# Attention, gated unit and softplus layer in one planned program: other transfer times, and slack on every VectorE and ScalarE instruction, in the simulation that makes the order

## The chip, the cores and the metric

The kernel runs on one core of one Trainium2 chip. The metric is the device time of one execution in microseconds. Shown with the program are the times of three runs, and one further execution that the hardware profiler took.

## What is computed

Three layers follow one another over 4 x 576 = 2304 tokens of 512 features, all in float32.

```
scores = q k^T / 8                      # 4 batches, 8 heads, 576 tokens, 64 features
mask: heads 0-3: 0 <= i - j < 32;  heads 4-7: j <= i and j = i (mod 32)
x = softmax(masked scores) v            # to 2304 x 512
xn = x / sqrt(mean(x^2) + 1e-6) * rms_g
y = (silu(xn w_gate) * (xn w_val)) w_out    # 512 -> 1536 -> 512
out = softplus(y w_in) w_out2               # 512 -> 2048 -> 512
```

## The kernel before

**The work.** The attention goes by units: a batch, a pair of heads, and about half of its query blocks (local heads have blocks of 64 queries and 96 keys, strided heads have blocks of 54, three residue classes of 18 tokens). A unit has a stage of scores (matmuls into one of four PSUM banks, VectorE's maximum, lines 555 to 588), of exponentials (ScalarE, one instruction per block, line 599), of normalisation, of transposes (line 637) and of values (line 660). In the two wide layers every float32 operand is split into a high and a low part, each product takes three matmuls with float32r operands (line 434), and 2 x 2 blocks of activations and weights are combined by sums and differences so that seven products stand for eight (`quad`). Tokens are worked in two sides, the first 1024 and the other 1280; the first side of the gated layer begins beside the attention.

**The weights.** They come as 64-bit words of 512 KB a tile. `decode` loads such a tile (line 369, buffers `raw`, a ring of two), makes float32 of it with one ScalarE and three VectorE instructions (lines 370 to 378) and stores it to `w_kept` (line 379), from where later sides fetch it (line 382).

**The order.** Tile's own scheduling is off. `Program.add` records each instruction as a node: engine, a duration in ns, what it reads and writes, and for a transfer the number `kb`. `Program.emit` then simulates the chip: `Trial.run` is a list scheduler in which each engine takes, among the nodes that are ready, the one that is due first; due times go back from the wanted order of TensorE. It does this 8 times, each time with the wanted times moved towards those that came out, keeps the trial that ends first, and issues the instructions in that order. Each engine of the chip then works its list from the front. There are two such plans: the attention with the first ten column groups of the gated layer, and all the rest.

What the simulation charges: VectorE 68 + n / 0.96 ns for n columns; ScalarE 15 + n / 0.98, and 236 + 0.83 n for an exponential with its accumulator read; a change between kinds of matmul 125 ns. Some instructions may go to another engine where the simulation finds it better: evictions to VectorE in place of ScalarE, and two-operand instructions to GpSimd when at least 900 ns of VectorE work stand ahead (`BESIDE`). A transfer takes SyncE 650 ns to issue; its data occupy one common queue for 5 ns per KB (`kb`), which starts 400 ns after the issue or when the transfer ahead is through, and it has landed 1100 ns after that:

```python
self.landed = max(self.landed, at + 400) + nodes[i][4]   # nodes[i][4] = 5 * kb
ends[i] = self.landed + 1100
```

Line numbers are those of the kernel before; a helper's line (355, 434) stands for all its callers.

Of the kernel before, what the change touches and what calls it, by code (L numbers as in the profile page):

```python
# [47 lines left out]

HOP = {"PE": 210, "DVE": 175, "ACT": 240, "POOL": 90, "SP": 60}
WINDOW = 3413  # L50
TURNS, KEEP, SWITCH, LEAVE = 8, 0.5, 125, 4000


class Program:
# [14 lines left out]

    def add(self, eng, dur, fn, r=(), w=(), kb=0, alt=None, mode=0):  # L70
        i = len(self.nodes)
        port = eng in ("DVE", "POOL") and not any("bank" in x[0] for x in [*r, *w])
        deps = set()
        for (key, lo, hi), wr in [(x, False) for x in r] + [(x, True) for x in w]:
            old = self.seen.setdefault(key, [])
            keep = []
            for e in old:
                if e[0] < hi and lo < e[1]:
                    if wr or e[3]:
                        deps.add(e[2])  # L80
                    if wr and lo <= e[0] and e[1] <= hi:
                        continue
                keep.append(e)
            keep.append((lo, hi, i, wr))
            self.seen[key] = keep
        deps.discard(i)
        self.nodes.append((eng, dur, fn, deps, 5 * kb, self.side, port, alt, mode))
# [40 lines left out]
class Trial:  # L128
# [7 lines left out]
    def pe_time(self, at, dur, mode):  # L136
        while at >= self.edge:
            used = self.acc / WINDOW
            if self.rate == 1 and used < 0.36:
                self.rate = 2  # L140
            elif self.rate == 2 and used > 0.75:
                self.rate = 1
            self.acc, self.edge = 0.0, self.edge + WINDOW
        t = (dur + (SWITCH if mode != self.mode else 0)) * self.rate
# [4 lines left out]
    def run(self):  # L149
        nodes, new, succ, ready, due, free = self.nodes, self.new, self.succ, self.ready, self.due, self.free  # L150
        begin, ends = self.begin, self.ends
# [16 lines left out]
        def release(i):  # L168
            for q in queues(i):
                heapq.heappush(wait[q], (ready[i], i))  # L170

        def earliest(q, base):
            for h in (wait[q], avail[q]):
                while h and h[0][1] in begin:
                    heapq.heappop(h)
            if avail[q]:
                return max(base, min(ready[i] for _, i in avail[q] if i not in begin))
            return max(base, wait[q][0][0]) if wait[q] else None
# [19 lines left out]
        while len(ends) < len(new):  # L198
            best = None

            def offer(at, e, s=0):
                nonlocal best
                if at is not None and (best is None or at < best[0]):
                    best = (at, e, s)

            first = [(t, q) for q in modes for t in [earliest(q, free["PE"])] if t is not None]
            if first:
                t = min(first)[0]
                pick = min((take(q, t)[0] + (LEAVE if q != self.mode else 0), q) for u, q in first if u <= t)
                offer(t, "PE", pick[1])  # L210
            offer(earliest("ACT", free["ACT"]), "ACT", "ACT")
            offer(earliest("SP", free["SP"]), "SP", "SP")
            t0, t1 = earliest("DVE0", free["DVE"]), earliest("DVE1", max(free["DVE"], self.port))
            if t0 is not None and t1 is not None and t0 == t1:
                offer(t0, "DVE", "DVE0" if take("DVE0", t0) < take("DVE1", t1) else "DVE1")
            else:
                offer(t0, "DVE", "DVE0")
                offer(t1, "DVE", "DVE1")
            base = max(free["POOL"], self.port)
            t = earliest("FLEX", base)  # L220
            if t is not None:
                beside = max(0, free["DVE"] - t) + sum(nodes[i][1] for _, i in avail["DVE0"])
                if beside >= BESIDE:
                    offer(t, "POOL", "FLEX")
            offer(earliest("POOL", base), "POOL", "POOL")
            at, e, s = best
            _, i = take(s, at)
            heapq.heappop(avail[s])
            if nodes[i][0] != e:
                nodes[i] = (e, nodes[i][7][0], nodes[i][7][1]) + nodes[i][3:]  # L230
            begin[i] = at
            free[e] = at + (self.pe_time(at, nodes[i][1], nodes[i][8]) if e == "PE" else nodes[i][1])
            ends[i] = free[e]
            if nodes[i][6]:
                self.port = free[e]
            if e == "SP":
                self.landed = max(self.landed, at + 400) + nodes[i][4]
                ends[i] = self.landed + 1100
            for j in succ[i]:
                gap = 0 if e == "PE" == nodes[j][0] else HOP[e]  # L240
                ready[j] = max(ready[j], ends[i] + gap)
                left[j] -= 1
                if not left[j]:
                    release(j)
# [3 lines left out]
def attn_glu_softplus(  # L248
# [13 lines left out]
    nc = tc.nc  # L262
    pr = Program()

    def all_of(key):
        return (key, 0, 1 << 30)
# [4 lines left out]
    def act(n, fn, r, w, table=False):  # L271
        pr.add("ACT", 15 + n / 0.98, fn, r + ([all_of("table")] if table else []), w)
# [14 lines left out]
    def dma(kb, fn, r, w):  # L287
        pr.add("SP", 650, fn, r, w, kb=kb)
# [23 lines left out]
    id_sb = const.tile([128, 128], F32, name="id_sb")  # L312
# [48 lines left out]
    hold = []  # L361

    def decode(src, t, kt, keep):

        raw, kraw = raws.next()
        u, ku = cvu.next()
        words = raw.bitcast(U32).rearrange("p (n two) -> p n two", two=2)
        wlo, whi = words[:, :, 0], words[:, :, 1]
        dma(512, lambda: nc.sync.dma_start(out=raw, in_=src), hold, [kraw])
        act(512, lambda: nc.scalar.activation(t, whi.bitcast(F32), AF.Copy, scale=2.0 ** -112), [kraw], [kt])  # L370
        dve(512, lambda: nc.vector.tensor_scalar(out=u, in0=t.bitcast(U32), scalar1=0x80000000, scalar2=None,
                                                 op0=ALU.bitwise_and), [kt], [ku], True)
        dve(512, lambda: nc.vector.scalar_tensor_tensor(  # L373
            out=u, in0=wlo, scalar=29, in1=u, op0=ALU.logical_shift_right, op1=ALU.bitwise_or),
            [kraw, ku], [ku])
        dve(512, lambda: nc.vector.scalar_tensor_tensor(
            out=t.bitcast(U32), in0=t.bitcast(U32), scalar=3, in1=u,
            op0=ALU.logical_shift_left, op1=ALU.bitwise_or), [kt, ku], [kt])
        dma(256, lambda: nc.sync.dma_start(out=wk[keep], in_=t), [kt], [("wk", keep, keep + 1)])

    def fetch(t, kt, keep):
        dma(256, lambda: nc.sync.dma_start(out=t, in_=wk[keep]), [("wk", keep, keep + 1)], [kt])
# [95 lines left out]
    def attention(at, use):  # L478
# [3 lines left out]

        qks = ring(at, "qk", 3, [128, 2 * QW])
        mask = at.tile([128, MW], BF16, name="mask")
        dma(100, lambda: nc.sync.dma_start(out=mask, in_=masks), [], [all_of("mask")])
        vb = ring(at, "vb", 2, [128, 9, 128])
        eb = ring(at, "eb", EB, [128, 5 * LK])
        pp = ring(at, "pp", 2, [128, 6, 128])
# [32 lines left out]
        def load_v(u):  # L521
            b, p, t0, n = units[u]
            kp, nt = (LK, 9) if p < 2 else (128, 6)
            vt, (kv, _, _) = vb.next()
            src = vl[b, p] if p < 2 else vs[b, p - 2]
            vals[u // 2] = (vt, kv)
            dma(nt * (48 if p < 2 else 50), lambda: nc.sync.dma_start(out=vt[:kp, :nt, :], in_=src), [], [all_of(kv)])

        def half(u, h):
            o = h ^ (u % 2)  # L530
# [116 lines left out]
        def stage_v(u):  # L647
            b, p, t0, n = units[u]
            loc = p < 2
            r0, r1 = (0, LK) if loc else (64, 64 + SK) if t0 else (0, SK)  # L650
            v0 = t0 if loc else 0
            vt, kv = vals[u // 2]
# [3 lines left out]
            for a in range(n):  # L656
                t, kt = pts[a // 3]
                for h in range(2):
                    o = (2 * (a % 3) + (h ^ (u % 2))) * nq
                    pr.add("PE", 59, lambda a=a, h=h, o=o, t=t: nc.tensor.matmul(  # L660
                        xb[64 * h:64 * h + 64, a * nq:(a + 1) * nq], lhsT=vt[r0:r1, v0 + a, 64 * h:64 * h + 64],
                        rhs=t[r0:r1, o:o + nq], start=True, stop=True), [all_of(kv), kt],
                        [kx], mode=1 if loc else 3)
            g = rg_sb[:, p:p + 1]
            if loc:
# [3 lines left out]
                src = xb[:, :w]  # L669
# [6 lines left out]
            else:  # L676
# [3 lines left out]
                src = xb[:, :w].rearrange("p (c m) -> p c m", m=18)  # L680
# [297 lines left out]
    with tc.manual_schedule():  # L978
# [38 lines left out]
                fn(*args)  # L1017
            pr.side = False

        dma(64, lambda: nc.sync.dma_start(out=id_sb, in_=ident), [], [all_of("id")])  # L1020
        dma(2, lambda: nc.sync.dma_start(out=rg_sb, in_=rg), [], [all_of("rg")])
        for i in range(WARM):
            pr.add("PE", 400, lambda: nc.tensor.matmul(
# [102 lines left out]
        for side, (c0, c1, c4) in enumerate(SIDES):  # L1126
# [3 lines left out]
            for p in range(n2):  # L1130
                i = prep2(p, c4 is not None, "POOL" if p == 0 or side == 0 and p < 4 else "DVE")
# [86 lines left out]
```

## Time and profile before

| what | value |
|---|---|
| median of 3 runs | 899.95 us (899.71 to 902.26) |
| the profiled execution | 900.52 us |
| its span, first to last instruction | 898.7 us |
| TensorE, VectorE, ScalarE, GpSimd busy | 882.7, 712.9, 486.1, 28.1 us |
| instructions | 14075 |
| mean granted TensorE clock | 0.993 |

Busy time is the union of an engine's instructions, without its waits. PE is TensorE, PEld its weight loads, DVE VectorE, ACT ScalarE, POOL GpSimd, SP SyncE, which issues all transfers. The ends of matmuls are modelled, so TensorE's busy time can hold small pauses. In a row of groups, "bank<-pt,vb" names the tile written and those read.

### The profile page before, as it was taken

The numbers are of one execution on the slowest core, as the hardware profiler recorded it, in microseconds if no ns is written. First come the engines' busy times: TensorE is split into PE (matmuls) and PEld (weight loads), VectorE is DVE, ScalarE is ACT, GpSimd is POOL, SyncE is SP. The second block draws the span as 40 slices with busy tenths as digits, with TensorE's granted clock in tenths as the row PEclk, the third lists the DMA queues.
The fourth block names the chain that finished last, engine by engine and source line by source line (L and its number), as shares of the span: only waits on it lengthen the run. The fifth ranks groups of instructions, "written<-read, shape, count | busy, mean of one in ns | idle before, by whom it ended". The sixth has DMA issues, their size and how long they took to land.

```text
span 898.7 us, 14075 instructions
## 1 busy us (share of the span) xinstructions
PE 882.7 (98%) x5320; PEld 725.7 (81%) x5320; DVE 712.9 (79%) x1349; ACT 486.1 (54%) x999; POOL 28.1 (3%) x26
## 2 busy tenths in 40 slices
PE   7899999999999999999999999999999999999998
PEld 6567777778777888888888888888888888888886
DVE  4988898998599995888988799877798456676644
ACT  5987664545364675444545567544474655434331
POOL 0000010200000000000100100000000000000000
PEclk7999999999999999999999999999999999999999
DMA  7874667363040443344553025321114111111003
GB/s 254 263 228 146 205 205 224 124 214 106 13 141 23 151 152 105 134 146 140 183 154 104 2 85 178 137 71 48 47 47 153 36 47 48 47 32 39 1 1 117
DMA packets 41858, 102.18 MB, mean 114 GB/s; under 512 B 4800, under 2 KB 5568, under 8 KB 41792
## 3 DMA queue, kind: packets, MB, share of 16 engines
q1 hardware_dynamic: 41792, 101.31, 35.5%
q8 instruction: 41, 0.67, 0.3%
q14 instruction: 25, 0.20, 0.1%
HBM read 78.74 MB, written 22.54 MB: 113 GB/s over the span
## 4 chain that ended last, share of the span: by engine, by line
PE 67%; DVE 3%; issue 0%
PE bank L434 67%; DVE xs L901 1%; DVE ob L355 0%; DVE tb L355 0%; DVE xs L355 0%; DVE win L355 0%; DVE w L355 0%; DVE ssq L355 0%; DVE glx L355 0%; DVE xs L919 0%; DVE gv L355 0%; DVE ssq L868 0%; DVE gv L868 0%; DVE gl L355 0%
## 5 line engine op out<-in xcount | busy, mean ns | idle before, releaser
L434 PE MATMUL bank<-ob,win 128*128 128x512 f32 (+1 forms) x1560 | 430.8, 360 | 2.7 <-ACT ob L351 1.8
L434 PEld LDWEIGHTS bank<-ob,win 128*128 128x128 f32 x1560 | 283.4, 188 | 55.0 <-ACT ob L351 2.2
L434 PE MATMUL bank<-tb,win 128*128 128x512 f32 x672 | 232.8, 392 | 0.0
L434 PEld LDWEIGHTS bank<-tb,win 128*128 128x128 f32 x672 | 125.4, 188 | 22.9 <-DVE xs L901 0.4
L919 DVE TENSOR_TENSOR xs<-bank,xs 128x512 f32<-128x512 f32 x126 | 86.8, 689 | 45.7 <-PE bank L434 44.4
L405 ACT ACTIVATE win<-w 128x512 fp32r<-128x512 f32 (+1 forms) x136 | 83.4, 616 | 63.9 <-PE bank L434 32.7
L355 DVE TENSOR_TENSOR win<-w,win 128x512 fp32r<-128x512 f32 (+1 forms) x134 | 89.5, 673 | 15.6 <-ACT win L405 12.6
L434 PE MATMUL bank<-wout,ghx 128*128 128x512 f32 x304 | 100.0, 390 | 0.0
L434 PE MATMUL bank<-wout,gh 128*128 128x512 f32 x272 | 90.4, 390 | 0.0
L434 PE MATMUL bank<-ghx,wout 128*128 128x512 f32 x224 | 84.1, 394 | 0.0
L434 PE MATMUL bank<-gh,wout 128*128 128x512 f32 (+1 forms) x256 | 81.3, 356 | 0.5 <-DVE xs L901 0.4
L901 DVE TENSOR_TENSOR xs<-bank,xs 128x512 f32<-128x512 f32 (+1 forms) x100 | 62.2, 628 | 8.9 <-PE bank L434 8.1
L434 PEld LDWEIGHTS bank<-wout,ghx 128*128 128x128 f32 x304 | 56.9, 188 | 11.7
L434 PEld LDWEIGHTS bank<-wout,gh 128*128 128x128 f32 x272 | 50.9, 188 | 10.6
L816 ACT ACTIVATE gv<-bank 128x512 f32<-128x512 f32 x48 | 28.4, 592 | 48.1 <-PE bank L434 47.6
L434 PE MATMUL bank<-wout,glx 128*128 128x512 f32 x152 | 53.2, 389 | 0.0
L434 PEld LDWEIGHTS bank<-gh,wout 128*128 128x128 f32 x256 | 45.5, 189 | 9.0 <-DVE xs L901 1.4
L434 PEld LDWEIGHTS bank<-ghx,wout 128*128 128x128 f32 x224 | 41.9, 188 | 8.4 <-ACT ghx L856 0.2
L434 PE MATMUL bank<-wout,gl 128*128 128x512 f32 x136 | 47.7, 389 | 0.0
L373 DVE SCALAR_TENSOR_TENSOR cvu<-raw,cvu 128x512 uint32<-128x512 uint32 x68 | 46.6, 686 | 1.0
L355 DVE TENSOR_TENSOR w<-w 128x256 f32<-128x256 f32 x109 | 45.4, 416 | 0.9
L820 DVE TENSOR_TENSOR gv<-bank,gv 128x512 f32<-128x512 f32 x48 | 32.9, 685 | 16.0 <-ACT gv L816 9.0
(131 smaller groups left out, 1211.8 us busy)
## 6 DMA issues: line engine op xcount, KB each, us to landing
raw<-w SPq DMA_DIRECT2D x68, 512.0 KB, 4.1
w<-w_kept SPq DMA_DIRECT2D x56, 256.0 KB, 2.6
w_kept<-cvtx SPq DMA_DIRECT2D x26, 256.0 KB, 3.7
cvt<-w_kept SPq DMA_DIRECT2D x26, 256.0 KB, 2.7
w_kept<-w SPq DMA_DIRECT2D x24, 256.0 KB, 4.2
qk<-qk SPq DMA_DIRECT2D x8, 601.0 KB, 5.6
w_kept<-cvt SPq DMA_DIRECT2D x18, 256.0 KB, 3.5
cvtx<-w_kept SPq DMA_DIRECT2D x18, 256.0 KB, 2.8
```

Of the source, the lines that this page charges most:

```text
L355: pr.add("DVE", 68 + n / 0.96, lambda: getattr(nc.vector, name)(o, x, y), r, w, alt=(110 + n * 2.3, lambda: getattr(nc.gpsimd, name)(o, x, ...
L373: dve(512, lambda: nc.vector.scalar_tensor_tensor(out=u, in0=wlo, scalar=29, in1=u, op0=ALU.logical_shift_right, op1=ALU.bitwise_or), [kra ...
L405: act(n, lambda: nc.scalar.activation(h, t, AF.Copy), [kt], [reg(0, o + lo, o + hi)])
L434: lambda a=a, b=b, i=i, st=st, mv=mv: nc.tensor.matmul(o, lhsT=st[a], rhs=mv[b], start=(first and i == 0), stop=(last and i == m - 1), ski ...
L816: act(CH, lambda: nc.scalar.activation(o, y[0], AF.Copy), [y[1]], [ko])
L820: dve(CH, lambda: nc.vector.tensor_add(o[0], y[0], o[0]), [y[1], o[1]], [o[1]])
L901: dve(n, lambda: nc.vector.tensor_add(x, pb, x), [kp, kx], [kx])
L919: dve(DM, lambda: nc.vector.tensor_add(x, pb, x), [kp, kx], [kx])
```

## The change

Only numbers of the simulation are edited. Each VectorE and ScalarE node gets 20 ns more. The `kb` of several kinds of transfers changes, and with it the time in the common queue: a raw weight tile 512 to 340, a store to `w_kept` 256 to 170, values 48 to 31 a block (local) and 50 to 41 (strided), the mask 100 to 140, the identity 64 to 40; the fetch from `w_kept` stays at 256, q and k at 0.35 a column. The landing delay of 1100 ns becomes 2110 for a raw tile, 1460 for a store, 1260 for all else; the two are told apart by their time in the queue. A strided value matmul is charged 36 ns in place of 59. What the instructions do stays the same; their order, and the engine of those that have a choice, follow from the new simulation.

```diff
--- before.py
+++ after.py
@@ -48,6 +48,7 @@
 
 HOP = {"PE": 210, "DVE": 175, "ACT": 240, "POOL": 90, "SP": 60}
 WINDOW = 3413
+SLACK = 20
 TURNS, KEEP, SWITCH, LEAVE = 8, 0.5, 125, 4000
 
 
@@ -69,6 +70,7 @@
 
     def add(self, eng, dur, fn, r=(), w=(), kb=0, alt=None, mode=0):
         i = len(self.nodes)
+        dur += SLACK if eng in ("DVE", "ACT") else 0
         port = eng in ("DVE", "POOL") and not any("bank" in x[0] for x in [*r, *w])
         deps = set()
         for (key, lo, hi), wr in [(x, False) for x in r] + [(x, True) for x in w]:
@@ -235,7 +237,7 @@
                 self.port = free[e]
             if e == "SP":
                 self.landed = max(self.landed, at + 400) + nodes[i][4]
-                ends[i] = self.landed + 1100
+                ends[i] = self.landed + (2110 if nodes[i][4] == 1700 else 1460 if nodes[i][4] == 850 else 1260)
             for j in succ[i]:
                 gap = 0 if e == "PE" == nodes[j][0] else HOP[e]
                 ready[j] = max(ready[j], ends[i] + gap)
@@ -366,7 +368,7 @@
         u, ku = cvu.next()
         words = raw.bitcast(U32).rearrange("p (n two) -> p n two", two=2)
         wlo, whi = words[:, :, 0], words[:, :, 1]
-        dma(512, lambda: nc.sync.dma_start(out=raw, in_=src), hold, [kraw])
+        dma(340, lambda: nc.sync.dma_start(out=raw, in_=src), hold, [kraw])
         act(512, lambda: nc.scalar.activation(t, whi.bitcast(F32), AF.Copy, scale=2.0 ** -112), [kraw], [kt])
         dve(512, lambda: nc.vector.tensor_scalar(out=u, in0=t.bitcast(U32), scalar1=0x80000000, scalar2=None,
                                                  op0=ALU.bitwise_and), [kt], [ku], True)
@@ -376,7 +378,7 @@
         dve(512, lambda: nc.vector.scalar_tensor_tensor(
             out=t.bitcast(U32), in0=t.bitcast(U32), scalar=3, in1=u,
             op0=ALU.logical_shift_left, op1=ALU.bitwise_or), [kt, ku], [kt])
-        dma(256, lambda: nc.sync.dma_start(out=wk[keep], in_=t), [kt], [("wk", keep, keep + 1)])
+        dma(170, lambda: nc.sync.dma_start(out=wk[keep], in_=t), [kt], [("wk", keep, keep + 1)])
 
     def fetch(t, kt, keep):
         dma(256, lambda: nc.sync.dma_start(out=t, in_=wk[keep]), [("wk", keep, keep + 1)], [kt])
@@ -482,7 +484,7 @@
 
         qks = ring(at, "qk", 3, [128, 2 * QW])
         mask = at.tile([128, MW], BF16, name="mask")
-        dma(100, lambda: nc.sync.dma_start(out=mask, in_=masks), [], [all_of("mask")])
+        dma(140, lambda: nc.sync.dma_start(out=mask, in_=masks), [], [all_of("mask")])
         vb = ring(at, "vb", 2, [128, 9, 128])
         eb = ring(at, "eb", EB, [128, 5 * LK])
         pp = ring(at, "pp", 2, [128, 6, 128])
@@ -524,7 +526,7 @@
             vt, (kv, _, _) = vb.next()
             src = vl[b, p] if p < 2 else vs[b, p - 2]
             vals[u // 2] = (vt, kv)
-            dma(nt * (48 if p < 2 else 50), lambda: nc.sync.dma_start(out=vt[:kp, :nt, :], in_=src), [], [all_of(kv)])
+            dma(nt * (31 if p < 2 else 41), lambda: nc.sync.dma_start(out=vt[:kp, :nt, :], in_=src), [], [all_of(kv)])
 
         def half(u, h):
             o = h ^ (u % 2)
@@ -657,7 +659,7 @@
                 t, kt = pts[a // 3]
                 for h in range(2):
                     o = (2 * (a % 3) + (h ^ (u % 2))) * nq
-                    pr.add("PE", 59, lambda a=a, h=h, o=o, t=t: nc.tensor.matmul(
+                    pr.add("PE", 59 if loc else 36, lambda a=a, h=h, o=o, t=t: nc.tensor.matmul(
                         xb[64 * h:64 * h + 64, a * nq:(a + 1) * nq], lhsT=vt[r0:r1, v0 + a, 64 * h:64 * h + 64],
                         rhs=t[r0:r1, o:o + nq], start=True, stop=True), [all_of(kv), kt],
                         [kx], mode=1 if loc else 3)
@@ -1017,7 +1019,7 @@
                 fn(*args)
             pr.side = False
 
-        dma(64, lambda: nc.sync.dma_start(out=id_sb, in_=ident), [], [all_of("id")])
+        dma(40, lambda: nc.sync.dma_start(out=id_sb, in_=ident), [], [all_of("id")])
         dma(2, lambda: nc.sync.dma_start(out=rg_sb, in_=rg), [], [all_of("rg")])
         for i in range(WARM):
             pr.add("PE", 400, lambda: nc.tensor.matmul(
```

## Rows read from the trace of the kernel before

**Rows 1.** Page, first part: busy us, share of the span, instructions of each engine.

```profile
PE 882.7 (98%) x5320; PEld 725.7 (81%) x5320; DVE 712.9 (79%) x1349; ACT 486.1 (54%) x999; POOL 28.1 (3%) x26
```

**Rows 2.** Windows by stage: stretch, its length, busy us (instructions) per engine, clock, DMA, GB/s.

```profile
0.00:22.50 22.50, 17.69 (x282) 14.79 (x285) 11.01 (x40) 13.18 (x76) 1.61 (x6) 0.79 0.76 254
22.50:45.00 22.50, 18.72 (x328) 12.96 (x322) 21.46 (x60) 20.92 (x91) 0.00 (x0) 0.98 0.83 264
45.00:67.50 22.50, 20.94 (x218) 15.22 (x218) 18.87 (x46) 19.66 (x57) 0.00 (x0) 1.00 0.72 228
67.50:90.00 22.50, 21.66 (x167) 15.83 (x166) 20.01 (x43) 17.22 (x30) 1.29 (x1) 1.00 0.47 144
90.00:247.50 157.50, 157.10 (x1218) 124.36 (x1217) 134.34 (x269) 82.49 (x148) 12.06 (x9) 1.00 0.50 156
247.50:292.50 45.00, 44.23 (x188) 34.66 (x187) 44.78 (x79) 25.57 (x44) 2.70 (x2) 1.00 0.27 82
292.50:877.50 585.00, 584.96 (x2864) 493.86 (x2863) 452.03 (x803) 304.19 (x554) 10.44 (x8) 1.00 0.28 88
877.50:898.70 21.20, 17.36 (x77) 14.06 (x75) 10.43 (x16) 2.87 (x5) 0.00 (x0) 0.96 0.33 124
```

**Rows 3.** Chain of work that ended last: start us, us, what.

```profile
272.56 0.60 DVE win L355
...
291.31 223.95 PE bank L434 x1172
...
515.30 379.58 PE bank L434 x1770
```

**Rows 4.** Waits of TensorE, 0 to 90 us: in total, times, longest.

```profile
PE bank L553 <- ACT eb L599: 3.3, 2, 2.9
PE bank L434 <- ACT ob L351: 1.8, 2, 1.4
PE bank L453 <- ACT eb L599: 1.4, 1, 1.4
...
PE bank L566 <- DMA qk<-qk: 0.7, 1, 0.7
```

**Rows 5.** Transfers issued at 20 to 75 us: count, KB each, median us to landing.

```profile
raw<-w SPq DMA_DIRECT2D x9, 512.0 KB, 4.0
vb<-v_loc SPq DMA_DIRECT2D x4, 432.0 KB, 6.3
vb<-v_str SPq DMA_DIRECT2D x4, 384.0 KB, 5.3
w_kept<-w SPq DMA_DIRECT2D x5, 256.0 KB, 5.4
qk<-qk SPq DMA_DIRECT2D x2, 608.0 KB, 6.7
qk<-qk SPq DMA_DIRECT2D x2, 601.0 KB, 7.0
w_kept<-cvt SPq DMA_DIRECT2D x1, 256.0 KB, 2.8
w_kept<-cvtx SPq DMA_DIRECT2D x1, 256.0 KB, 3.0
```

**Rows 6.** Window 20 to 75 us, columns as in rows 2.

```profile
20.00:75.00 55.00, 49.21 (x611) 34.64 (x611) 46.86 (x118) 49.03 (x174) 0.00 (x0) 0.97 0.75 237
```

**Rows 7.** Line 369, loads of raw weights, all 68.

```profile
DMA to landing us min/median/max: 3.2/4.1/7.8
```

**Rows 8.** Groups of instructions by line and form: the strided value matmuls.

```profile
L660 PE MATMUL bank<-pt,vb 54*64 54x54 f32 x352 | 9.0, 234 | 0.0
```

**Rows 9.** Waits of SyncE's queue: us in total, times, longest.

```profile
SPq L369 <- DVE cvu L373: 188.4, 58, 11.9
```

**Rows 10.** Two windows of the start, columns as in rows 2.

```profile
6.80:13.40 6.60, 2.98 (x108) 2.53 (x100) 4.68 (x15) 4.88 (x33) 0.00 (x0) 0.97 1.05 337
13.40:20.00 6.60, 6.46 (x94) 5.02 (x93) 4.63 (x19) 4.54 (x28) 0.00 (x0) 0.50 0.50 187
```

## The prediction

> **What bounds the kernel now.** I read the page's first part first: TensorE is busy 98% of the span, VectorE 79%, ScalarE 54% [rows 1]. A share over the whole span hides stages, so the busy time of each engine by stage came next [rows 2]. There the reader sees two kernels in one. From 292.5 to 877.5 us TensorE is busy 584.96 of 585.00 us at full clock; from 90 to 292.5 us it is idle 157.50 - 157.10 + 45.00 - 44.23 = 1.17 us. Only the first 90 us, the attention with the first weights decoded beside it, have room: 4.81 us idle up to 22.5 us, then 3.78, 1.56 and 0.84 us, together 10.99 us; 6.18 us of it lie between 22.5 and 90 us. The last 21.2 us hold 3.84 us, the tail behind the last matmul.
>
> The chain of work that ended last agrees [rows 3]: from 291.3 us on it is TensorE alone, 1172 + 1770 matmuls in two unbroken pieces, 223.95 us / 1172 = 191 ns and 379.58 us / 1770 = 214 ns each, short and long ones mixed. No order of the same matmuls shortens that. Just before it a run of VectorE instructions follows one another every 0.60 us.
>
> Third, what TensorE waited for in the first 90 us [rows 4]. The named waits are on ScalarE (the exponentials, the Square of the statistics, the splits of activations) and on VectorE; one, of 0.7 us, is on a transfer. So the place to win is the order of ScalarE's and VectorE's work before 90 us, and these two are themselves nearly full there: in 22.5 to 45 us VectorE has 1.04 us left and ScalarE 1.58 us, in 45 to 90 us 6.12 and 8.12 us [rows 2].
>
> **The change, part by part.** It edits only numbers by which the planner simulates; no instruction is added or removed in any kind. A number counts by the order it yields: the chip runs at its own speed, and each engine works in the order written.
>
> *Transfers.* Old charge per KB: 5 ns for most, for q and k 0.35 x 5 ns a column. I price the stretch 20 to 75 us by the transfers issued there [rows 5]. Nine raw weights x 512 x 5 = 2.56 us make 23.04; four local values x 9 x 48 x 5 = 2.16 make 8.64; four strided x 6 x 50 x 5 = 1.50 make 6.00; seven stores (5 + 1 + 1) x 1.28 make 8.96; four q-k loads at 2.13 (1216 columns) and 2.10 (1202 columns) make 8.46. Sum 55.1 us in a stretch of 55.0: in the plan the transfers are saturated there, so data are planned to come later and later. New: 9 x 1.70 + 4 x 1.395 + 4 x 1.23 + 7 x 0.85 + 8.46 = 15.30 + 5.58 + 4.92 + 5.95 + 8.46 = 40.2 us, 73%. The trace has the DMA engines at 0.75 in that stretch, 237 GB/s [rows 6]. So the new charge is right and the old one invented a queue. A raw weight alone is planned to land 0.40 + 2.56 + 1.10 = 4.06 us after its issue by the old numbers, 0.40 + 1.70 + 2.11 = 4.21 by the new; the row has 3.2 at least and 4.1 in the median [rows 7]. Alone nothing moves; behind others the new plan brings the data forward by up to 55.1 - 40.2 = 14.9 us summed over the stretch, less where a buffer has to come free first.
>
> What is that worth? Nothing directly, for transfers hardly stop TensorE. Indirectly: decoding is placed on ScalarE and VectorE where the plan thinks that the weight is there. Placed earlier it fills their gaps, and what follows it comes earlier. In 45 to 90 us both have room (6.12 and 8.12 us), so TensorE's 2.40 us of idle time could all go; in 22.5 to 45 us its 3.78 us could shrink by no more than the room of the fuller pair, 1.04 to 1.58 us. Lower bound 0, upper 2.40 + 1.58 = 3.98 us. I take the middle, 2.0 us, because room on an engine is not yet work that is ready for it.
>
> *Slack.* Each VectorE and ScalarE instruction is charged 20 ns more. A VectorE instruction over 512 columns was charged 68 + 512 / 0.96 = 601 ns; the chain shows one every 0.60 us [rows 3]. So the old charge was right and 621 is too long. Over the 60 + 46 + 43 = 149 VectorE instructions of 22.5 to 90 us [rows 2] the plan sees 3.0 us that don't exist; over ScalarE's 178 at most 3.6 us (an exponential and its accumulator read share one charge). The chip gives that time back as soon as it runs. What it changes is which work is held to be late: where the plan had no margin, it now has 20 ns for every instruction ahead. Good for: the 1.17 us of idle time in 90 to 292.5 us, which VectorE, full there (44.78 of 45.00 us), causes. Bad for: a fuller VectorE in the plan sends more subtractions to GpSimd. I put slack at 0, with bounds of 1.17 us gained and, for a loss, the new wait priced below.
>
> [...]
>
> *The strided value matmuls*, 59 ns charged before, 36 now. The row has 352 records [rows 8], two for each of 8 head pairs x 11 blocks x 2 halves = 176 charges; the plan loses 176 x 23 ns = 4.0 us of TensorE time over the attention. The row's 9.0 us / 176 = 51 ns lies between, 8 below the old and 15 above the new. Real TensorE time doesn't change by it; I take 0, bounds within those of the order. The other small charges (mask, identity, landing of stores and fetches later by 0.16 us in light traffic) move a plan that had spare time there: 0. If that cover went, the 0.7 us on a transfer [rows 4] is the nearest price.
>
> **Sum.** The profiled execution took 900.52 us, its span 898.7 with 1.82 around it; it lies 0.57 above the median, 899.95. I take the 2.0 us off the median: 897.95, say 898.0.
>
> **Rivals.**
>
> *Nothing comes of it.* The plan is truer, but in the raw buffers' ring of two the next load waits for VectorE anyway: 58 of the raw loads waited for the decoding instruction that frees their buffer, 188.4 us in all [rows 9]. Then transfers never were what set the decoding, the engines are as full as before, and the order changes only in detail. Against it: the plan's queue was saturated, which must have moved some decoding back. Time: 899.95.
>
> *A larger gain.* All idle time from 22.5 to 292.5 us goes, 6.18 + 1.17 = 7.35 us: 892.6. For it: every wait there is for ScalarE or VectorE work that a better order could have put first. Against it: VectorE busy 21.46 of 22.5 us. Half of it or more counts here, 896.3 and below.
>
> *Slower: a new wait in the attention.* With 20 ns more for every exponential and reduction, and weights planned earlier, a decoding step (about four instructions of 0.6 us) stands ahead of an exponential chain in ScalarE's or VectorE's order. TensorE's score matmuls then find no free bank. Its price is the longest such wait in the rows, 2.9 us [rows 4]: 899.95 + 2.9 = 902.9. It decides when it exceeds the 2.0 us won, that is with two decoding instructions or more on top of that. For it: ScalarE and VectorE are 93 to 95% full at 22.5 to 45 us, where each instruction put first delays another. [...]
>
> **How the numbers follow.** Within 0.3%, that is 2.7 us (897.25 to 902.65), a measurement of this kernel can hardly tell a change. The gain of about 2 us, my forecast, has 0.45; its own bounds are 899.95 - 3.98 = 896.0 and 899.4, so it splits into 0.20 faster and 0.25 within 0.3%. Nothing: 0.20, all within. The larger gain: 0.15, all faster. Slower: 0.20, of which 0.17 lie beyond the 0.3%. Faster 0.35, same 0.48, slower 0.17. For 8 in 10 the range reaches into both outer cases: low 893.5, short of the full 7.35 us; high 903.0, the new wait.
>
> **What would show it.** Right: from 22.5 to 90 us TensorE idle some 4 us instead of 6.18; raw loads and decodings earlier in that stretch; from 292 us on the same unbroken matmul chain, starting about 2 us earlier; the clock as before. The slack is right if the small waits at 247.5 to 292.5 us (0.77 us) shrink, wrong if GpSimd's busy time grows well above 28.1 us [rows 1] and VectorE waits for it. The forecast is wrong if idle time before 90 us is 11 us or more again, if a wait of 2 us or more stands at a score or statistics matmul, or if TensorE has idle time behind 292 us, where I left it none.

## The result

The changed kernel takes 906.80 us in the median of 5 runs (904.29 to 906.98) against 900.63 us (899.71 to 902.26, 5 runs) before: ratio 1.0057, 95% interval 1.0043 to 1.0071 (ratios here compare all executions, not the medians). It is slower, outside the range that I gave, and on the other side of the forecast. The profiled execution has a span of 904.9 us against 898.7.

The busy time by stage, changed kernel, columns and stretches as in [rows 2]:

```profile
0.00:22.50 22.50, 15.06 (x289) 13.18 (x289) 11.58 (x42) 13.36 (x76) 1.61 (x6) 0.92 0.90 307
22.50:45.00 22.50, 18.38 (x272) 12.94 (x274) 18.26 (x52) 19.10 (x78) 0.80 (x1) 0.81 0.68 219
45.00:67.50 22.50, 21.02 (x190) 16.01 (x182) 18.81 (x50) 15.67 (x54) 4.17 (x1) 0.81 0.55 171
67.50:90.00 22.50, 21.25 (x168) 14.75 (x167) 19.51 (x37) 17.36 (x32) 0.00 (x0) 1.00 0.63 199
90.00:247.50 157.50, 156.63 (x1230) 124.08 (x1231) 132.95 (x267) 83.22 (x149) 14.56 (x13) 1.00 0.48 154
247.50:292.50 45.00, 45.00 (x236) 36.68 (x231) 43.08 (x74) 26.08 (x44) 1.29 (x1) 1.00 0.25 76
292.50:877.50 585.00, 584.50 (x2860) 493.20 (x2859) 458.66 (x810) 306.88 (x559) 16.14 (x11) 1.00 0.28 88
877.50:904.90 27.40, 23.22 (x103) 18.89 (x101) 13.79 (x21) 3.54 (x6) 0.00 (x0) 0.97 0.26 96
```

TensorE's idle time in the first 90 us is 7.44 + 4.12 + 1.48 + 1.25 = 14.29 us; it was 10.99. The 6.2 us more of span divide so: 3.30 us of idle time in the first 90 us, 0.47 in 90 to 247.5 us, 0.46 behind 292.5, 0.34 in the tail, less 0.77 gained at 247.5 to 292.5; together 3.80 us. The other 2.4 us are busy time: 885.06 against 882.66 us for the same 5320 matmuls. The clock column goes with it: 0.81 in two stretches, where it was 0.98 and 1.00 (in the first 22.5 us it is the other way, 0.92 where it was 0.79).

Waits of TensorE from 0 to 90 us, changed kernel, as in [rows 4] (L555 starts a bank of scores with the mask, L639 is a transpose):

```profile
PE bank L555 <- ACT eb L601: 6.5, 3, 4.8
PE bank L639 <- DVE eb L357: 1.7, 1, 1.7
```

Its longest wait, for exponentials that free a bank of scores, went from 2.9 to 4.8 us. The chain of work that ended last, changed kernel, shows it and, much later, a second place:

```profile
7.96 1.43 ACT eb L601 x10
9.65 3.42 ACT eb L601 x21
13.11 0.54 PE bank L555 x2
...
423.69 4.59 DMA w_kept<-cvtx
...
432.42 468.31 PE bank L436 x2230
```

The chain waits through 31 ScalarE records (exponentials and accumulator reads) up to 13.11 us. At 432 us TensorE stood still for the 0.5 us that the last large window lacks; from there it is unbroken as in [rows 3].

The longer first wait goes with another order of the first two head pairs. TensorE's first score matmuls, before (96 columns: the local pair) and then changed (54 columns: the strided pair):

```profile
5.86 1.47 PE L566 MATMUL bank<-qk 64*64 64x96 f32 x36
```

```profile
5.87 1.08 PE L568 MATMUL bank<-qk 64*64 64x54 f32 x46
```

TensorE at half clock, changed kernel, three windows set on the stretches:

```profile
22.80:26.20 3.40, 3.15 (x61) 2.67 (x63) 2.25 (x11) 2.67 (x10) 0.00 (x0) 0.50 0.47 135
33.10:36.50 3.40, 3.40 (x5) 1.30 (x4) 2.23 (x6) 2.40 (x11) 0.00 (x0) 0.50 0.93 298
43.30:53.50 10.20, 9.28 (x55) 7.01 (x55) 10.20 (x24) 6.11 (x18) 4.97 (x1) 0.50 0.40 125
```

In the profiled execution of before there was one such stretch ahead of the tail, which [rows 10] show in part; the window set on the whole of it:

```profile
13.00:23.20 10.20, 10.06 (x154) 8.18 (x156) 7.18 (x25) 8.12 (x52) 0.00 (x0) 0.50 0.66 233
```

The changed kernel has one of its own between 12.6 and 16 us, and then these three more, with TensorE busy 3.15 + 3.40 + 9.28 = 15.83 us in them.

How much of this belongs to the order, and not to the one execution? Two kernels of the experiments, "second plan new" and "second plan, slack only", keep the first plan of before: in the first 90 us their matmuls, and their VectorE instructions, follow one another by tile names as before. Yet their profiled executions show half clock at 11.4 to 18.2 us (11.5 to 18.4) and once more at 45.5 to 48.9 (45.7 to 49.1). The second one, "second plan new":

```profile
45.50:48.90 3.40, 3.40 (x10) 2.67 (x9) 3.40 (x9) 2.29 (x11) 0.00 (x0) 0.50 0.51 111
```

So where half clock falls is not set by the order alone, and TensorE's busy time in the first 90 us, 79.01 us before, was 77.43 and 76.42 us in these two; a difference of two or three microseconds between two profiles can be one of executions, the 3.30 us above too. The sum of half clock separates the orders better: some 10.2 us in all three executions of the old first plan, 20.4 us in the changed kernel, 23.8 us in the other profiled execution of its first plan ("first plan new").

The six statistics matmuls show what half clock means. Timeline of TensorE, before:

```profile
30.19 3.12 PE L453 MATMUL bank<-gv,ones 128*128 128x512 f32 x6 [1.43 <-ACT eb L599]
```

and the same six in the changed kernel, line 455 there, where the granted clock is 0.50 from 33.1 to 36.5 us:

```profile
32.58 4.54 PE L455 MATMUL bank<-gv,ones 128*128 128x512 f32 x6 [1.19 <-ACT eb L601]
```

The sign that I gave for the transfers appeared. SyncE's timeline, first raw weights, before and then changed:

```profile
20.39 0.89 SPq L369 DMA_DIRECT2D raw<-w  x2
```

```profile
8.67 0.90 SPq L371 DMA_DIRECT2D raw<-w  x2
```

They are issued 12 us earlier, though not because a raw tile is charged less, as the experiments show. The decoding step on VectorE that reads the raw tile, its nine instructions in the first 90 us, first and last start, before and then changed:

```profile
L373 DVE SCALAR_TENSOR_TENSOR cvu<-raw,cvu x9: 677/692/693, 31.5 to 89.2; 128x512 uint32<-128x512 uint32 x9
```

```profile
L375 DVE SCALAR_TENSOR_TENSOR cvu<-raw,cvu x9: 675/692/693, 28.7 to 75.9; 128x512 uint32<-128x512 uint32 x9
```

The ninth starts 13 us earlier. So weights came sooner, and the attention beside them came later: its last value matmul starts at 248.0 us, before at 240.6.

### The profile page after: what moved, and what is told of

Its sections match the earlier page's. It is cut to its first block, busy times and chain, and to the rows that moved or that the text cites. A ratio compares the mean times of both kernels' runs of the same rounds, so it can differ in the third digit from the quotient of the medians.

```text
span 904.9 us, 14102 instructions
## 1 busy us (share of the span) xinstructions
PE 885.1 (98%) x5320; PEld 729.7 (81%) x5320; DVE 716.6 (79%) x1348; ACT 485.2 (54%) x994; POOL 38.6 (4%) x32
## 4 chain that ended last, share of the span: by engine, by line
PE 92%; DVE 4%; DMA 2%; ACT 1%; issue 0%; SPq 0%; ACTq 0%; DVEq 0%
PE bank L436 86%; PE bank L662 2%; PE bank L639 1%; PE bank L568 1%; PE bank L455 1%; ACT eb L601 1%; DMA raw<-w 1%; DMA w_kept<-cvtx 1%; PE bank L555 0%; DMA mask<-masks 0%; DMA vb<-v_loc 0%; DVE xs L474 0%; DVE cvu L375 0%; DVE mz L583 0%; DVE win L357 0%
## 5 line engine op out<-in xcount | busy, mean ns | idle before, releaser
L357 DVE TENSOR_TENSOR win<-w,win 128x512 fp32r<-128x512 f32 (+1 forms) x130 | 86.1, 667 | 20.2 <-ACT win L407 18.0
L436 PEld LDWEIGHTS bank<-gh,wout 128*128 128x128 f32 x256 | 45.5, 189 | 8.6 <-issue 0.9
```

The costliest lines, as they stand in the source:

```text
L357: pr.add("DVE", 68 + n / 0.96, lambda: getattr(nc.vector, name)(o, x, y), r, w, alt=(110 + n * 2.3, lambda: getattr(nc.gpsimd, name)(o, x, ...
L436: lambda a=a, b=b, i=i, st=st, mv=mv: nc.tensor.matmul(o, lhsT=st[a], rhs=mv[b], start=(first and i == 0), stop=(last and i == m - 1), ski ...
```

## The experiments

Theory A says that the new transfer numbers turned the first two head pairs round, and that this is the loss; theory B that the slack spoils the order; theory C that any newly made order lands some tenths of a per cent off. Each kernel was timed 5 to 12 times beside the kernel before on the same chip. For the kernels without idle matmuls, the table sets the ratio beside two readings of the first 90 us: TensorE's busy time and mean clock. The ratio comes from all executions, the readings from the single profiled one: before, "second plan new" and "second plan, slack only" share one first plan and read 76.42 to 79.01, and the 130 ns control's 0.98 is that of its fastest execution, with a granted clock of 0.998 over the span where the other ten had 0.994 to 0.996.

| kernel | ratio, 95% interval | busy in 0:90 | clock in 0:90 |
|---|---|---|---|
| before | 1 | 79.01 | 0.94 |
| changed | 1.0057 [1.0043, 1.0071] | 75.71 | 0.89 |
| no slack | 1.0048 [1.0035, 1.0062] | 74.91 | 0.92 |
| slack only | 1.0019 [1.0007, 1.0031] | 73.61 | 0.92 |
| second plan new | 0.9972 [0.9961, 0.9984] | 77.43 | 0.94 |
| second plan, slack only | 0.9984 [0.9973, 0.9994] | 76.42 | 0.94 |
| first plan new | 1.0089 [1.0071, 1.0108] | 75.83 | 0.87 |
| first plan, slack only | 1.0042 [1.0029, 1.0054] | 74.22 | 0.92 |
| first plan, transfers only | 1.0054 [1.0040, 1.0067] | 75.05 | 0.91 |
| first batch's values alone | 1.0022 [1.0010, 1.0034] | 76.12 | 0.91 |
| changed, first batch's values old | 1.0040 [1.0026, 1.0055] | 76.69 | 0.91 |
| control, 120 ns | 1.0027 [1.0015, 1.0038] | 76.00 | 0.92 |
| control, 130 ns | 0.9991 [0.9982, 1.0000] | 78.00 | 0.98 |

**Slack or transfers.** First the changed kernel without its slack:

```diff
-SLACK = 20
+SLACK = 0
```

> The changed kernel with the slack at 0 and all else as changed. Theory A (the transfer numbers turn the first two head pairs round: the strided pair's scores come first, its exponentials are mixed with those of the local pair, TensorE's first wait for a free bank grows from 2.9 to 4.8 us, and TensorE then falls to half clock more often): the turn stays, first wait 4.5 us or more, 903 to 907 us against 900.6 of before. Theory B (the slack spoils the order; the transfer numbers are harmless): first wait about 2.9 us, 898 to 901 us. Theory C (any newly made order lands some microseconds off, no number is to blame): anything from 896 to 907.

1.0048: most of the loss stays, with a first wait of 5.4 us. Then the slack alone on the kernel before (both lines of the change that name SLACK):

> The kernel before with the slack of 20 ns alone. Theory A: the local pair stays first, first wait 2.9 to 3.2 us, 899 to 902 us. Theory B: 904 to 907 us, with new waits of TensorE between 22.5 and 90 us. Theory C: anything from 896 to 907.

1.0019. Neither theory's number holds: the slack loses something too, less than theory B asks. The reason came with the plans taken apart.

**Which plan.** A flag gives the new numbers to one plan only:

```diff
-        dur += SLACK if eng in ("DVE", "ACT") else 0
+        dur += SLACK if self.new and eng in ("DVE", "ACT") else 0
...
+        pr.new = True      # between the two plans; the transfers' kb and delays likewise
```

> Old numbers in the first plan (attention and the first ten column groups), all new ones in the second. Theories A and B: the loss is made in the first plan, so this runs as before, 899.5 to 902 us, with TensorE unbroken from 292 us on. If the second plan has a part in it: 902 us or more, with idle time of TensorE behind 247 us.

> All new numbers in the first plan, the old ones in the second. The second plan alone gave 0.28% back. If the two parts add, this loses 0.57 + 0.28 = 0.85%, some 908 us beside 901; if the second plan's part rests on where the first one ends, it is like the changed kernel, 905 to 907 us.

> The kernel before with the slack of 20 ns in the second plan alone. If the slack made the 0.28% that the second plan gives back: 0.9960 to 0.9985 of before. If the transfer numbers made it: 0.999 to 1.001.

The second plan gains: 0.9972. I had expected no change. The first loses 1.0089, and 0.89 - 0.28 = 0.61% is close to the 0.57% of the whole. In the second plan the slack alone gives 0.9984. In both cases TensorE's idle 0.77 us at 247.5 to 292.5 us is gone (as in all eight kernels with slack in the second plan; the ten others keep 0.26 to 0.87 us), here for the slack alone:

```profile
247.50:292.50 45.00, 45.00 (x198) 36.87 (x197) 44.61 (x79) 26.39 (x45) 4.01 (x3) 1.00 0.26 83
```

That is 0.09% of the time; where the rest of the second plan's gain comes from these profiles don't show. In the first plan both halves lose:

> The kernel before with the slack of 20 ns in the first plan alone. Theory B in the form that is left (the slack harms the attention's order): 1.004 or more. If it is no worse than a control: 1.001 to 1.0035.

> The kernel before with all new transfer numbers and the 36 ns in the first plan alone, no slack. Theory A: the turned pairs, a first wait of 4.5 us or more, and with no gain of the second plan in it 1.005 to 1.008. If it is no worse than a control: 1.001 to 1.0035.

0.42% for the slack, 0.54% for the transfers with the 36 ns; the sum, 0.96%, is about the 0.89% of both. Both lie in the ranges that theories B and A had named. Whether each number loses by what it says or only by making another order, the controls below decide in part.

**The turned pairs.** One number of the kernel before, for the first of four batches:

```diff
-            dma(nt * (48 if p < 2 else 50), ...
+            dma(nt * ((31 if b == 0 else 48) if p < 2 else 50), ...
```

> The kernel before with one number changed: the local values of the first batch are charged 31 a block instead of 48. No transfer takes longer by it; it shifts the due times, so that the strided pair is loaded and scored first. Theory A: first wait 4.5 us or more and 902 to 905 us. Theory B: 899.5 to 901.5 us, since the slack is not in it. Theory C: anything from 896 to 907.

It turns the two pairs (80 score matmuls of 54 columns come first) and makes TensorE's first wait 5.1 us. Waits of TensorE from 0 to 90 us:

```profile
PE bank L553 <- ACT eb L599: 5.9, 3, 5.1
```

Due times run back through a transfer by twice its time. The local pair's banks, buffers and values are used again by the next local pair, whose values are now charged 1.5 us less in that count (17 x 9 x 5 = 765 ns, twice), so the first local pair is due later, and the strided pair goes first. That last step is read from the code; that this number alone does it, the run shows. Among the kernels of the table the turn and the longer first wait go together without exception: 4.7 to 5.4 us in the five turned ones, 1.8 to 3.2 us in the others. This order loses 0.22%, no more than the 120 ns control below.

The kernel also answers for the early weights: a raw tile is charged as before in it, and the first is issued at 8.85 us, as in the changed kernel (8.67). And the other way round:

> The changed kernel with the values of the first batch charged as before (48 and 50 a block), so that the local pair is scored first again; everything else as changed. Theory A (the turned pairs are the larger part of the loss in the first plan): first wait 3.2 us or less and 901 to 903 us, half of the changed kernel's loss or more gone. Theory C (any new order of the attention loses): 904 us or more although the first wait is short.

The first wait is 2.7 us again, and 0.57 - 0.40 = 0.17% comes back, less than half; the two intervals overlap, so that this difference alone is not clear of noise. Theory A's times, 901 to 903 us, were missed (904.12); that the turn is the larger part is not borne out.

**The clock.** Idle matmuls of ones into unused columns of a transpose bank, put where the plan has TensorE wait:

```diff
+                if spent is not None and at < 60000 and at - spent > 500:
+                    for _ in range(int((at - spent - 250) / 215)):
+                        self.filler()      # 128x128 of ones
```

> The changed kernel's order, with idle matmuls of ones into a free PSUM corner put where its plan has TensorE wait 0.5 us or more before 60 us; they compute nothing that is used. [...]

> The order of the kernel before with the same idle matmuls in its plan's waits. Half clock there lies at 13.0 to 23.2 us, where the exponentials set the pace: 0 to 1.5 us come back, 899.5 to 901 us. If half clock costs in full wherever it stands: 4 us or more, 897 us or below.

> The control of 120 ns with idle matmuls in the plan's waits before 60 us. If the loss of a newly made order is mostly half clock: 0.9985 to 1.0005, as the filled kernel before (0.9986). If it is mostly waits: 1.0015 or more.

> The changed kernel with the first batch's values charged as before (local pair first) and with idle matmuls in the plan's waits before 60 us. If turned pairs and half clock are two separate parts of the loss: 1.0020 of the filled kernel less the 0.0017 of the turn, 0.999 to 1.001 of before. If they are one cause (the turn brings the half clock): 1.001 to 1.003, as filled alone.

The changed order, filled, takes 1.0020 (1.0008 to 1.0031): 0.37% back, some 3.3 us. Its first 90 us, filled, columns as in [rows 2]; TensorE's busy time holds the fillers:

```profile
0.00:90.00 90.00, 84.42 (x1075) 66.64 (x1076) 71.55 (x186) 68.67 (x245) 7.89 (x8) 1.00 0.72 226
```

The clock is 1.00 and the six statistics matmuls take 3.19 us. VectorE and ScalarE, without any idle work of theirs, are busier (71.55 and 68.67 us, against 68.15 and 65.49 unfilled), as they would be if TensorE at half clock had kept them waiting. The order of before gains 0.14% by filling (0.9986, 0.9975 to 0.9998), the control 0.24% (1.0027 to 1.0003). With the first values old and filled, 1.0025 (1.0013 to 1.0038) is as good as filled alone: the turn and the half clock don't add, and beside the fillers the turn costs nothing that shows (though this kernel's clock was 0.92 from 67.5 to 90 us).

Since the order of before gains by filling too, the clock's share of the difference is smaller than 0.37%: with both filled, 901.91 us stand against 898.74 on one chip, and 1.0020 / 0.9986 leaves 0.34% (by the two intervals 0.18 to 0.50) of the 0.57%. So a good part of the loss, by these figures more than half, is not undone by holding the clock. In these two the last value matmul starts at 243.3 and 238.7 us: the attention is later at full clock too.

**Controls.** The charge for a change of matmul kinds has nothing to do with the change:

```diff
-TURNS, KEEP, SWITCH, LEAVE = 8, 0.5, 125, 4000
+TURNS, KEEP, SWITCH, LEAVE = 8, 0.5, 120, 4000
```

> A control that has nothing to do with the change: the kernel before with 120 ns charged for a change of matmul kinds instead of 125. Theory C (the attention's order is so fragile that any number moves the time by some tenths of a per cent): outside 0.998 to 1.002 of before. Otherwise within it.

> A second control: the kernel before with 130 ns for a change of matmul kinds. If newly made orders scatter both ways around the one of before: 0.997 to 1.003, and as likely below 1 as above. If the order of before is one of the better ones that this planner can hit: above 1.001 again, as with 120 ns (1.0027).

5 ns less lose 0.27%, 5 ns more gain 0.09%. Theory C has a part: the attention's order is fragile, and a single number unrelated to the change is worth a quarter of a per cent. Its first 90 us for 120 and then for 130 ns:

```profile
0.00:90.00 90.00, 76.00 (x968) 55.83 (x969) 69.12 (x179) 67.92 (x244) 3.48 (x8) 0.92 0.67 216
```

```profile
0.00:90.00 90.00, 78.00 (x992) 57.20 (x993) 73.53 (x191) 70.81 (x248) 6.04 (x11) 0.98 0.71 224
```

The new first plan's 0.89% (1.0071 to 1.0108) lies clearly outside what the two controls did. Its halves don't: the slack's interval (1.0029 to 1.0054) overlaps that of 120 ns (1.0015 to 1.0038), that of the transfers (1.0040 to 1.0067) begins just above it, and two controls don't give the whole spread. That the slack, or the turn, loses by its own working and not as any newly made order may, is not shown.

**A better version.** New raw-tile numbers alone in the first plan, all new ones in the second, and the fillers:

> Towards a better version: in the first plan only the raw weight tile's numbers are new, in the second plan all are; idle matmuls fill the first plan's waits before 60 us. If the gains add (0.28% of the second plan, 0.14% of the fill): 0.994 to 0.997 of before, some 896 us. If the first plan made newly is again off by chance: 0.998 or more.

0.9961 (0.9948 to 0.9974), 897.34 us beside 900.96: faster than before, and so than the changed kernel, by about what second plan and fill gave singly (0.28 + 0.14 = 0.42%). The raw tile's numbers seem to add nothing: the first raw weights are issued at 18.70 us and the ninth decoded at 87.0, where the filled kernel before has 18.94 and 87.4.

## Why the prediction was wrong

**What bounds the kernel: right.** TensorE from 292.5 to 877.5 us has 584.50 us of work in 585.00. What changed most changed in the first 90 us.

**Transfers: the sign came in part by luck, the step from there failed.** Raw weights are issued 12 us sooner and the ninth decoded 13 us sooner, but not since the plan's queue got shorter for them: the raw tile's numbers alone move neither (18.70 and 87.0 us), and the first batch's local values' charge alone brings the early issue (8.85 us). The ninth comes at 83.7 us by the new transfer numbers of the first plan without slack, and at 75.9 only with it. The step that failed is "I take the middle, 2.0 us": that work placed earlier on ScalarE and VectorE fills their gaps, and TensorE's gaps close behind it. The runs show the opposite sign: the new transfer numbers with the 36 ns, in the first plan alone, lose 0.54%, and from 22.5 to 90 us TensorE of the changed kernel is idle 6.85 us, where I forecast some 4. I took room on an engine for room that decoding would fill. In 22.5 to 45 us VectorE is now busy 18.26 us where it was 21.46, ScalarE 19.10 where it was 20.92: emptier, not fuller. Filled they are at 20.64 and 21.28 us, which fits that they wait for a TensorE that stands longer at the start and runs at half clock; but with the transfers alone they are at 20.32 and 20.38 us, hardly emptier, and the loss is there. So the sign is shown, its whole cause is not.

In the same sum the gain's upper time, 899.4 us, does not follow from its lower bound of 0, which gives 899.95.

**That due times move with a transfer's charge I left out.** I priced the queue's time alone. One such charge turned the first two pairs, and with the turn TensorE's first wait went from 2.9 to 4.8 us.

**Slack: 0 was wrong in the first plan (0.42% lost, if not as any new order may), and the bound of 1.17 us gained held in kind in the second**, where the idle 0.77 us went. My sign for a harmful slack, more GpSimd work, did not tell: GpSimd rose to 38.6 us in the changed kernel, but it rose to 36.1 us in the kernel with the second plan new, which is faster.

**The strided value matmuls at 36 ns** were not tried apart from the transfers in the first plan; their 0 stays open.

**The slower rival had the mechanism in part.** A longer wait at a score matmul, priced at 2.9 us more, came as 4.8 - 2.9 = 1.9 us more. Beside it stood more half clock: 2.4 us of extra busy time in the profile, and 3.3 us back when filled, 2.1 us of it beyond what the order of before got back (0.37 - 0.14 = 0.23%); the mean clock of the first 90 us is 0.89 in the changed kernel and 1.00 in the filled one. But I put the cause with decoding ahead of exponentials, where the longer first wait came with the turned pairs, gave the whole rival 0.20 of the chance, and ended the range at the wait alone. At 22.5 to 45 us TensorE's idle time hardly tells its clock: 3.78 us of it went with 0.98 before, and only 0.34 us more go with 0.81 in the changed kernel.

**Left open:** what makes the 0.34% that stays when both orders are filled; why the newly made orders of the attention were worse, all but the 130 ns control and perhaps the one with the raw tile's numbers alone, which ran only with fillers and the new second plan (the planner knows of half clock by a rule of its own, which was not varied); and most of the second plan's gain.

## What to carry to other kernels

Another cost in a greedy planner, even one meant to be truer, is a new order, not a better one: run controls that move an unrelated number by a little before crediting or blaming the change. A sign that was forecast counts only if the forecast cause made it: take that cause alone. Where an engine is idle at the start, ask whether it waits for the one that you mean to help; then its idle time is no room. Where the profile shows TensorE at half clock, idle matmuls in the waits can be worth as much as a better order (0.37% here with the clock of the first 90 us from 0.89 to 1.00, 0.14% with 0.94 to 1.00), and they show the clock's share if both orders are filled and compared.

## What the runs showed of the hardware that was not expected

The same order gets more or less half clock from one execution to the next, and its time follows. Over 98 executions of the kernel before, the mean granted clock of the span lies between 0.992 and 0.998: the 12 at 0.992 took 901.89 to 904.16 us, the 10 at 0.997 and 0.998 took 898.00 to 899.57. The changed kernel's five had 0.988 to 0.992 and took less at 0.992 (904.29 and 904.95 us) than at 0.988 and 0.989 (906.80 to 906.98).

Half clock cost much less than its length. The order of before, with some 10.2 us of it, got 0.14% back by filling, some 1.3 us; the changed kernel, with 20.4 us, got 0.37% back, some 3.3 us. Half the length, my estimate of the price if TensorE had work all through these stretches at the granted 0.50, would be 5.1 and 10.2 us. Whether the two late stretches of the changed kernel, 33.1 to 36.5 and 43.3 to 53.5 us, with TensorE busy 3.40 of 3.40 and 9.28 of 10.20 us, cost more than the early ones is not shown, for the fillers removed all at once. The mean clock of the whole span differs by 0.005 between the two profiles (0.993 and 0.988); the stage's own column (0.81) shows where.
